# Attention output copied from fixed buffers ahead of the state update, with shorter loads of k and q, in a kernel of attention and two MoE layers

## The chip, the cores and the metric

The kernel runs on one core of one Trainium2 chip, in one launch. Time is device microseconds of one execution of the whole program; before the change the median of 3 runs is 924.24 us (924.11 to 925.05).

## The reference

The first stage is a linear recurrence over a sequence of 768 positions, for 4 batches and 8 heads of 48 dimensions, with a decay `alpha` of its own for each key dimension and position:

```python
def _attn_ref(q, k, v, alpha):
    B, H, S, D = q.shape
    state = np.zeros((B, H, D, D), dtype=np.float32)
    y = np.zeros_like(q)
    for t in range(S):
        state = alpha[:, :, t, :, None] * state + np.einsum('bhd,bhe->bhde', k[:, :, t], v[:, :, t])
        y[:, :, t] = np.einsum('bhd,bhde->bhe', q[:, :, t], state)
    return y
```

Its output, transposed to 3,072 tokens of 384 features, goes through two layers of the form `act(x @ w_in) @ w_out` with 2,048 inner features. The first has a rational function of `h` as `act` (a cubic over `1 + |b0 h| + |b1| h²`), the second `h * cos(h)`. The change touches the first stage alone.

## The kernel before

**Attention in steps.** The sequence is cut into 6 chunks of 128 positions; with 4 batches that makes 24 steps u (chunk u // 4, batch u % 4). One tile of a step holds all 8 heads: 4 head pairs along the free axis, and on the 128 rows one head of a pair on rows 0 to 47, the other on rows 64 to 111. Rows 48 to 63 and 112 to 127 are filling. A step loads `a` (the decays), `kq` (k and q together, 128 rows × 1,024 numbers, 512 KB) and `v`. VectorE makes running products `p` of the decays (`decay`, L255) and, from a first guess on ACT (`guess`, L271), their inverse (`inverse0`, `inverse1`, L280 and L288); POOL scales k and q by these (`scale_k` L294, `scale_q` L299). Then:

- PE: `scores` (L307) makes k·q of the chunk in two PSUM tiles; ACT copies them out (`mask0`, L314), POOL zeroes the upper triangle (`mask1`, L319).
- PE: `transposes` (L327) turns k; ACT copies it out as `kt` (`k_out`, L332); PE multiplies it with v into `u` (`update0`, L339); VectorE adds that to the state and decays it by `pc` (`update1`, L349 to L353; `pc` comes from `last_decay`, L264).
- PE: the output is state times q (`y_state`, L372) plus scores times v (`y_scores`, L382), in one PSUM bank `b1`; ACT copies it to SBUF (`y_out`, L393) and SP stores it to DRAM as two DMAs of 48 rows (`y_store`, L399), from where the layers load it as `x`.

**Order of the work.** Every engine works through its instructions in the order in which they are written. The turns n = −3 to 24 (L1238) call `attention(n)` (L403), which writes pieces of several steps: scores, mask0 and transposes of step n; k_out, mask1, y_state, y_scores, update0 and y_out of step n−1; the decays of step n+3; the second half of the update of step n−2. Turn n also issues on SP, in this order, `a` of step n+5 (two DMAs of 48 rows, L233), `kq` of n+3 (L229), `v` of n+2 (L224), a piece of the weights (L149) and the store of step n−2 (L399). SP's DMAs have eight completion counters that are used in turn, so an issue waits until the eighth DMA before it has landed. In between ACT, VectorE and POOL unpack the weights (`tick`: L68, L69, L73, L74; `w_hi` L188; `w_lo` L198). From turn 20 (`LEAD`) on the two layers run beside the last attention steps.

**Buffers.** `temp(tag)` (L92) hands out buffers of a pool in turn; the tag `g` has four. In the attention stage `kt` (L331) and the output copy `yo` (L390) of each step both come from it, two copies a step. In 13 of the steps 0 to 19 (3 to 6, 9 to 13, 16 to 19) `yo` gets the buffer that `kt` of its own step has just left, in the others one that an earlier store has read. A writer of a buffer waits until everything that read it is done: the readers of a `kt` are the matmuls of `update0`, those of a `yo` are the two DMAs of its store. For u from 20 on `yo` comes from another pool. The `kq` tiles are five fixed buffers used in turn.

Of the kernel before, what the change touches and what calls it, by code (L numbers as in the profile page):

```python
# [16 lines left out]
B, H, S, D = 4, 8, 768, 48  # L17
DM, DFF = 384, 2048
NC, C = 6, 128
HP = 4  # L20
# [19 lines left out]
def attn_then_two_moe(ctx, tc, kqT, aT, vP, w1i, w1o, ma, mb, w2i, w2o, out):  # L40
    nc = tc.nc
# [50 lines left out]
    def temp(tag, dtype=F32, shape=(128, TB)):  # L92

        bufs = {"z": 3, "ah": 2, "g": 4, "hi": 3, "lo": 3}[tag]
        return el.tile(list(shape), dtype, tag=tag, name=tag, bufs=bufs)

    def bank(tag, shape=(128, TB), dtype=F32):

        return ps.tile(list(shape), dtype, tag=tag, name=tag)
# [28 lines left out]
    LEAD = NU - 4  # L128
# [52 lines left out]
    def w_hi():  # L181
        while to_hi:
            m, s, i = w = to_hi.pop(0)
            at = early(m, s, i)
            hi = ws[s][i][:, 0]
            if at is not None:
                hi = kq_t[at % 3][:, 1].rearrange("p a b -> p (a b)")[:, :DM].bitcast(F32R)
            nc.scalar.activation(out=hi, in_=stage[w], func=AF.Copy)  # L188
            to_lo.append((w, hi))
# [21 lines left out]


    U = {}

    def load(u, name):


        if u >= NU:
            return
        c, b = divmod(u, B)  # L220
        ts = {"a": a_t, "kq": kq_t, "v": v_t}[name]
        t, src = ts[u % len(ts)], {"a": aT, "kq": kqT, "v": vP}[name][c, b]
        if name == "v":
            nc.sync.dma_start(out=t[:, :H * D], in_=src)  # L224
        elif u == 0 and name == "a":
            for cs in (slice(0, HP + HP // 2 * C), slice(HP + HP // 2 * C, HP * (C + 1))):
                nc.sync.dma_start(out=t[:, cs], in_=src[:, cs])
        elif u < len(ts) or name == "kq":
            nc.sync.dma_start(out=t, in_=src)  # L229
        else:  # L230
            for j in range(2):
                js = slice(64 * j, 64 * j + D)
                nc.sync.dma_start(out=t[js], in_=src[js])  # L233
        d = U.setdefault(u, {})
        if name == "kq":
            d["k"], d["q"] = t[:, 0], t[:, 1]
        else:
            d[name] = t


    def parts(u):
        return [slice(0, HP // 2), slice(HP // 2, HP)] if u == 0 else [slice(0, HP)]
# [6 lines left out]
    def decay(u):  # L249
        d = U[u]  # L250
        d["p"] = in_p.tile([128, HP, C], F32, tag="p", name="p")
        a = d.pop("a")
        first, rest = a[:, :HP].unsqueeze(2), a[:, HP:].rearrange("p (a b) -> p a b", a=HP)
        for hs in parts(u):
            nc.vector.tensor_tensor(out=fresh[:, hs, 0:1], in0=first[:, hs], in1=fresh[:, hs, 1:2], op=ALU.max)  # L255
            nc.vector.tensor_tensor_scan(
                d["p"][:, hs].rearrange("p a b -> p (a b)"), rest[:, hs].rearrange("p a b -> p (a b)"),
                fresh[:, hs].rearrange("p a b -> p (a b)"), 0.0, ALU.mult, ALU.max,
            )

    def last_decay(u):
        d = U[u]
        d["pc"] = in_p.tile([128, HP, 1], F32, tag="pc", name="pc", bufs=6)
        nc.vector.tensor_tensor(out=d["pc"], in0=d["p"][:, :, C - 1:], in1=fresh[:, :, 1:2], op=ALU.max)  # L264


    def guess(u):
        d = U[u]
        d["r"] = bank("b1" if u == 1 else "r0", (128, HP, C))
        for hs in parts(u):  # L270
            nc.scalar.activation(out=d["r"][:, hs], in_=d["p"][:, hs], func=AF.Ln)  # L271
            nc.scalar.activation(out=d["r"][:, hs], in_=d["r"][:, hs], func=AF.Exp, scale=-1.0)
# [3 lines left out]
    def inverse0(u, hs):  # L276
        d = U[u]
        if hs.start == 0:
            d["m"] = temp("ah", shape=(128, HP, C))
        nc.vector.scalar_tensor_tensor(  # L280
            d["m"][:, hs], d["p"][:, hs], RANGE, d["r"][:, hs], ALU.min, ALU.mult, accum_out=sums(1, u, hs)
        )

    def inverse1(u, hs):
        d = U[u]
        if hs.start == 0:
            d["n"] = temp("z", shape=(128, HP, C))
        nc.vector.scalar_tensor_tensor(  # L288
            d["n"][:, hs], d["m"][:, hs], -2.0, d["r"][:, hs], ALU.add, ALU.mult, accum_out=sums(0, u, hs)
        )  # L290

    def scale_k(u, hs, eng):
        d = U[u]
        eng.tensor_tensor(out=d["k"][:, hs], in0=d["k"][:, hs], in1=d["n"][:, hs], op=ALU.mult)  # L294

    def scale_q(u):
        d = U[u]
        for hs in parts(u):
            nc.gpsimd.tensor_tensor(out=d["q"][:, hs], in0=d["q"][:, hs], in1=d["p"][:, hs], op=ALU.mult)  # L299

    def scores(u):
        d = U[u]
        d["sc"] = [ps_acc.tile([128, HP, C], F32, tag=f"acc{j}", name=f"sc{j}") for j in range(2)]
        for hp in range(HP):
            for j in range(2):
                js = slice(64 * j, 64 * j + D)
                nc.tensor.matmul(d["sc"][j][:, hp, :], d["k"][js, hp, :], d["q"][js, hp, :], start=True, stop=True)  # L307

    def mask0(u):
        d = U[u]  # L310
        d["s"] = []
        for j, sc in enumerate(d.pop("sc")):
            s = temp(("hi", "lo")[j], shape=(128, HP, C))
            nc.scalar.activation(out=s, in_=sc, func=AF.Copy, scale=-1.0)  # L314
            d["s"].append(s)

    def mask1(u):
        for s in U[u]["s"]:
            nc.gpsimd.affine_select(  # L319
                s, s, pattern=[[0, HP], [1, C]], compare_op=ALU.is_ge, fill=0.0, base=0, channel_multiplier=-1  # L320
            )
# [6 lines left out]

    def k_out(u):
        d = U[u]  # L330
        d["kt"] = temp("g", shape=(128, HP, 128))  # L331
        nc.scalar.activation(out=d["kt"], in_=d.pop("tp"), func=AF.Copy)  # L332

    def update0(u):
# [42 lines left out]
    def y_scores(u):  # L377
        c, b = divmod(u, B)
        d = U[u]
        for hp in range(HP):  # L380
            for j in range(2):
                nc.tensor.matmul(  # L382
                    d["y"][64 * j:64 * j + 64, hp, :], d["v"][:, (2 * hp + j) * D:(2 * hp + j) * D + 64], d["s"][j][:, hp, :],
                    start=not c and hp == 0, stop=True, skip_group_check=True,
                )

    def y_out(u):
        d = U[u]
        if u < NU - B:
            d["yo"] = temp("g", shape=(128, HP, C))  # L390
        else:
            d["yo"] = in_p.tile([128, HP, C], F32, tag="p", name="yo")
        nc.scalar.activation(out=d["yo"], in_=d["y"], func=AF.Copy)  # L393
# [9 lines left out]
    def attention(n, tick):  # L403

        def on(u, more=False):
            return 0 <= u < (NU - B if more else NU)

        whole = slice(0, HP)
        if on(n - 1, True):
            k_out(n - 1)  # L410
        w_hi()

        if on(n):
            scores(n)

        if 0 <= n - 1 < LEAD:
            mask1(n - 1)
        if on(n + 1):
            scale_q(n + 1)

        if on(n + 1):
            if n < 1:
                for hs in parts(n + 1):
                    inverse0(n + 1, hs)
                    inverse1(n + 1, hs)
                    scale_k(n + 1, hs, nc.gpsimd)
            else:
                inverse0(n + 1, whole)
                inverse1(n + 1, whole)
                scale_k(n + 1, whole, nc.vector if n + 2 == NU else nc.gpsimd)  # L430
                tick(0 if on(n + 2) else 1)
        tick(1)
        if on(n + 3):
            decay(n + 3)
        tick(1)
        if on(n - 2, True):
            update1(n - 2, tick)
        tick(1)
        if on(n + 3):
            last_decay(n + 3)  # L440

        if on(n):
            mask0(n)
        if n not in (-1, 0) and on(n + 2):
            guess(n + 2)
        if n in (-2, -1):
            guess(n + 3)

        if on(n - 1):
            y_state(n - 1)  # L450
            y_scores(n - 1)
        if on(n, True):
            transposes(n)
        if on(n - 1, True):
            update0(n - 1)
        if on(n - 1) and n < LEAD:
            y_out(n - 1)
        tick(1 if n < LEAD else 2)
        if on(n) and n >= LEAD:
            mask1(n)  # L460
# [760 lines left out]
    with tc.manual_schedule():  # L1221
        nc.scalar.preload_act_table_set("natural_log_exp_and_others")
        for name, u in (("a", 0), ("a", 1), ("kq", 0), ("kq", 1)):
            load(u, name)
# [239 lines left out]
```

## Time and profile before

| | |
|---|---|
| median of 3 runs | 924.24 us (924.11 to 925.05) |
| the profiled execution, its own time | 924.49 us |
| its span in the profile | 922.8 us |
| PE busy over the span | 895.2 us, 97% |
| ACT, POOL, DVE busy | 697.5, 712.5, 706.6 us (76, 77, 77%) |
| PE's matmul clock, mean of full speed | 0.995 |
| q1, the DMA queue of the program's transfers | 122.95 MB, 41.7% of 16 engines' time |

The busy shares are means over the whole program. Attention takes the first eighth or so of the span and the two layers the rest; these have different limits, so a change in attention has to be read from that stretch alone. The profile names a wait by the instruction that waited and by what ended the wait; times in the trace count from the start of the span.

### The profile page before, as it was taken

To read this page: it belongs to the slowest core of one execution; us is meant where nothing else is said; L and a number is where in the kernel's file an instruction comes from. 1 tells how busy PE (TensorE), PEld (TensorE's weight loads), DVE (VectorE), ACT (ScalarE), POOL (GpSimd) and SP (SyncE) were. 2 spreads that over 40 slices of the span, in tenths; PEclk is the share of its full clock that TensorE was granted. 3 is DMA by queue.
4 is the path that set the end of the run, shared out by engine and by line. 5 is a ranking of instruction groups with operands and counts; after the bars stand their busy time and mean duration, and the time that the engine had idled before them with its cause. 6 is when DMAs were issued, how large, how long until landed. Compare 5 with 4: busy or idle time off the path is not lost.

```text
span 922.8 us, 15700 instructions
## 1 busy us (share of the span) xinstructions
PE 895.2 (97%) x5336; PEld 741.7 (80%) x5336; DVE 706.6 (77%) x1246; ACT 697.5 (76%) x1305; POOL 712.5 (77%) x699
## 2 busy tenths in 40 slices
PE   7888899999999999999999999999999999999996
PEld 6776678888888888888888888878888888888885
DVE  7888979998999989979979967666367554555552
ACT  6998888888789878888878778755577676666653
POOL 6998998998889879889979758758887475665332
PEclk8999999999999999999999999999999999999999
DMA  9999940011124133142157457541243433533432
GB/s 298 315 310 311 329 137 16 28 35 52 68 78 121 43 100 97 46 150 89 34 163 223 140 185 260 195 136 35 69 138 94 154 116 100 171 104 103 138 103 90
DMA packets 64313, 124.04 MB, mean 134 GB/s; under 512 B 7424, under 2 KB 29184, under 8 KB 64224
## 3 DMA queue, kind: packets, MB, share of 16 engines
q1 hardware_dynamic: 64224, 122.95, 41.7%
q8 instruction: 44, 0.72, 0.3%
q14 instruction: 45, 0.37, 0.1%
HBM read 93.04 MB, written 29.88 MB: 133 GB/s over the span
## 4 chain that ended last, share of the span: by engine, by line
PE 86%; DMA 5%; ACT 4%; DVE 2%; issue 1%; POOL 1%; SPq 0%; ACTq 0%; DVEq 0%; POOLq 0%
PE acc L522 28%; PE b L506 28%; PE acc L987 15%; PE b L952 6%; PE r L952 5%; DMA x0d<-g 2%; DMA spare<-w1o 1%; PE b L1131 1%; DMA raw<-w1o 1%; PE sc L307 1%; DMA kq<-kqT 1%; DMA raw<-w1i 1%; ACT st L68 0%; ACT g L332 0%; ACT hi L314 0%
## 5 line engine op out<-in xcount | busy, mean ns | idle before, releaser
L506 PE MATMUL b<-x,w 128*128 128x512 f32 x1143 | 287.6, 396 | 0.2 <-DVE g L575 0.2
L506 PEld LDWEIGHTS b<-x,w 128*128 128x128 f32 x1143 | 214.4, 188 | 52.3 <-DVE g L575 0.6
L522 PE MATMUL acc<-hi,w 128*128 128x512 f32 x738 | 252.7, 396 | 0.0
L557 POOL TENSOR_TENSOR lo<-g,hi 128x512 fp32r<-128x512 f32 x128 | 174.5, 1363 | 69.5 <-ACT hi L552 63.2
L522 PEld LDWEIGHTS acc<-hi,w 128*128 128x128 f32 x738 | 138.7, 188 | 34.1
L1044 POOL TENSOR_TENSOR lo<-g,hi 128x512 fp32r<-128x512 f32 x64 | 83.0, 1297 | 103.8 <-ACT hi L1043 91.8
L522 PE MATMUL acc<-lo,w 128*128 128x512 f32 x369 | 145.6, 395 | 0.0
L552 ACT ACTIVATE hi<-g 128x512 fp32r<-128x512 f32 x128 | 80.8, 631 | 85.3 <-DVE g L588 47.4
L583 POOL TENSOR_TENSOR z<-z,ah 128x512 f32<-128x512 f32 x96 | 126.5, 1318 | 8.0
L987 PE MATMUL acc<-hi,w_out 128*128 128x512 f32 x384 | 130.4, 396 | 0.0
L584 DVE TENSOR_TENSOR g<-g,b 128x512 f32<-128x512 f32 x96 | 65.3, 680 | 26.5 <-ACT g L581 26.1
L522 PEld LDWEIGHTS acc<-lo,w 128*128 128x128 f32 x369 | 69.4, 188 | 16.4
L987 PE MATMUL acc<-lo,w_out 128*128 128x512 f32 x192 | 76.3, 398 | 0.4 <-POOL lo L1044 0.2
L987 PEld LDWEIGHTS acc<-hi,w_out 128*128 128x128 f32 x384 | 68.6, 188 | 9.9
L582 POOL TENSOR_SCALAR z<-ah,cq 128x512 f32<-128x512 f32 x96 | 74.5, 776 | 1.0 <-ACT ah L580 0.9
L581 ACT ACTIVATE g<-b,cq 128x512 f32<-128x512 f32 x96 | 74.6, 777 | 0.0
L588 DVE SCALAR_TENSOR_TENSOR g<-g,cq,r 128x512 f32<-128x512 f32 x96 | 70.8, 737 | 0.1
L575 DVE SCALAR_TENSOR_TENSOR g<-g,cq,b 128x512 f32<-128x512 f32 x96 | 70.6, 735 | 0.0
L592 ACT ACTIVATE r<-z,lnb 128x512 f32<-128x512 f32 x96 | 66.7, 695 | 0.9 <-POOL z L583 0.9
L577 DVE SCALAR_TENSOR_TENSOR r<-z,r 128x512 f32<-128x512 f32 x96 | 65.5, 683 | 0.0
L572 DVE SCALAR_TENSOR_TENSOR z<-z,r 128x512 f32<-128x512 f32 x96 | 64.9, 676 | 0.0
L580 ACT ACTIVATE ah<-b 128x512 f32<-128x512 f32 x96 | 56.4, 588 | 8.0 <-PE b L506 7.0
(192 smaller groups left out, 1823.3 us busy)
## 6 DMA issues: line engine op xcount, KB each, us to landing
w_out<-wd SPq DMA_DIRECT2D x64, 384.0 KB, 3.0
kq<-kqT SPq DMA_DIRECT2D x24, 512.0 KB, 5.4
raw<-w2i SPq DMA_DIRECT2D x16, 384.0 KB, 3.5
w<-wd SPq DMA_DIRECT2D x16, 384.0 KB, 3.3
raw<-w2o SPq DMA_DIRECT2D x16, 384.0 KB, 3.5
wd<-w SPq DMA_DIRECT2D x16, 384.0 KB, 2.6
v<-vP SPq DMA_DIRECT2D x24, 192.0 KB, 5.4
x<-x0d SPq DMA_DIRECT2D x18, 256.0 KB, 3.7
```

Source lines behind the costliest of these rows:

```text
L506: nc.tensor.matmul(h, ws[0][f][:, w, ks], x[:, xx, kk, :], start=i == 0, stop=i == 8)
L522: nc.tensor.matmul(acc[k], ws[1][f][:, w, ks], d[g], start=first and i == 0, stop=last and i == 2)
L552: nc.scalar.activation(out=t["hi"], in_=t["g"], func=AF.Copy)
L557: eng.tensor_tensor(out=t["lo"], in0=t["g"], in1=t["hi"].bitcast(F32), op=ALU.subtract)
L575: nc.vector.scalar_tensor_tensor(g, g, cq[:, 3:4], two["h"], ALU.add, ALU.mult)
L581: nc.scalar.activation(out=g, in_=h, func=AF.Identity, scale=cq[:, 5:6], bias=cq[:, 4:5])
L582: nc.gpsimd.tensor_scalar(zz, ah, cq[:, 1:2], cq[:, 0:1], ALU.mult, ALU.add)
L583: nc.gpsimd.tensor_tensor(out=zz, in0=zz, in1=ah, op=ALU.mult)
L588: nc.vector.scalar_tensor_tensor(g, g, cq[:, 2:3], r, ALU.add, ALU.mult)
L952: nc.tensor.matmul(tile[:, half], w[p], x[q], start=start and i == 0, stop=True, skip_group_check=True)
L987: nc.tensor.matmul(acc[k], item["w"][:, w, ks], item[g], start=first, stop=last)
L1044: nc.gpsimd.tensor_tensor(out=p["lo"], in0=p["g"], in1=p["hi"].bitcast(F32), op=ALU.subtract)
```

## The change

Four things are edited. (1) Four buffers `kept` are taken from the `g` pool once, at the start. (2) `k_out` writes `kept[0]` and `kept[1]` in turn. (3) `y_out` writes `kept[2]` and `kept[3]` in turn (for u below 20), and its call in `attention` stands ahead of `transposes` and `update0`, for n below `LEAD`. (4) The `kq` loads from u = 5 on, that is from the second use of each of the five buffers, load rows 0 to 111 alone (64 + 48); rows 112 to 127 keep what the buffer's first load left there.

```diff
     U = {}
+    kept = [temp("g", shape=(128, HP, C)) for _ in range(4)]
...
-        elif u < len(ts) or name == "kq":
+        elif u < len(ts):
             nc.sync.dma_start(out=t, in_=src)
+        elif name == "kq":
+            rows = slice(0, 64 + D)
+            nc.sync.dma_start(out=t[rows], in_=src[rows])
         else:
...
     def k_out(u):
         d = U[u]
-        d["kt"] = temp("g", shape=(128, HP, 128))
+        d["kt"] = kept[u % 2]
...
     def y_out(u):
         d = U[u]
         if u < NU - B:
-            d["yo"] = temp("g", shape=(128, HP, C))
+            d["yo"] = kept[2 + u % 2]
...
         if on(n - 1):
             y_state(n - 1)
             y_scores(n - 1)
+        if on(n - 1) and n < LEAD:
+            y_out(n - 1)
         if on(n, True):
             transposes(n)
         if on(n - 1, True):
             update0(n - 1)
-        if on(n - 1) and n < LEAD:
-            y_out(n - 1)
```

In the changed kernel `k_out` is L336, `mask0` L318, `y_out` L397, the `kq` load L233 and `y_store` L403.

On every engine the instructions stand in the same order before and after. What differs is what they wait for. ACT in turn 17, before: `hi` and `lo` are the two score copies of step 17, `r0` the guess of step 19, `g_1605` the output copy of step 16, `x` a piece of layer input, `g_1616` the `kt` copy of step 17, `w1_7` and `st` weights. In brackets stand the counters waited for: PE, DVE, Pool and Activation are engines, DMAHW0 to DMAHW7 the eight counters of SP's DMAs.

```order
L314 ACTIVATE hi_1567<-sc0_1538 128x512 [waits PE_49]
L314 ACTIVATE lo_1569<-sc1_1539 128x512 [waits PE_49]
L271 ACTIVATE r0_1571<-p_1476 128x512 [waits DVE_49]
L272 ACTIVATE r0_1571<-r0_1571 128x512 [waits Activation_49]
L393 ACTIVATE g_1605<-b1_1574 128x512 [waits PE_49]
L635 ACTIVATE x_794<-x_794 128x512 [waits DMAHW4_49]
L332 ACTIVATE g_1616<-b0_1591 128x512 [waits DMAHW7_49,DMAHW0_49]
L188 ACTIVATE w1_7_128<-st_104 128x384 [waits DVE_49]
L68 ACTIVATE st_104<-spare_141 128x384 [waits DMAHW6_49,Pool_49]
```

The same place after:

```order
L318 ACTIVATE hi_1538<-sc0_1509 128x512 [waits PE_49]
L318 ACTIVATE lo_1540<-sc1_1510 128x512 [waits PE_49]
L275 ACTIVATE r0_1542<-p_1449 128x512 [waits DVE_49]
L276 ACTIVATE r0_1542<-r0_1542 128x512 [waits Activation_49]
L397 ACTIVATE g_144<-b1_1545 128x512 [waits DMAHW7_49,DMAHW6_49,PE_49]
L639 ACTIVATE x_784<-x_784 128x512 [waits DMAHW4_49]
L336 ACTIVATE g_143<-b0_1563 128x512 [waits PE_49]
L188 ACTIVATE w1_7_128<-st_104 128x384 [waits DVE_49]
L68 ACTIVATE st_104<-spare_141 128x384 [waits Pool_49]
```

The output copy of step 16 waited for PE up to the last matmul of `update0(16)`; now it waits for PE up to `y_scores(16)`, and on two DMA counters for the landing of store(14), which read `kept[2]` last. The `kt` copy of step 17 waited for the landing of store(13), and by way of it for all that PE had done; now it waits for the transposes of step 17. On SP one turn (turn 13: the loads of `kq` of step 16 and `v` of step 15, a weight piece, the store of step 11) reads, before:

```order
L229 DMA kq_99<-kqT 128x1024 [waits DMAHW5_49,PE_49,Pool_49]
L224 DMA v3_103<-vP 128x384 [waits DMAHW6_49,PE_49]
L149 DMA spare_141<-w1o 128x768 [waits DMAHW7_49]
L399 DMA x0d_57<-g_1193 48x512 [waits DMAHW0_49,Activation_49]
L399 DMA x0d_57<-g_1193 48x512 [waits DMAHW1_49]
```

and after:

```order
L233 DMA kq_99<-kqT 112x1024 [waits DMAHW5_49,PE_49,Pool_49]
L225 DMA v3_103<-vP 128x384 [waits DMAHW6_49,PE_49]
L149 DMA spare_141<-w1o 128x768 [waits DMAHW7_49]
L403 DMA x0d_57<-g_145 48x512 [waits DMAHW0_49,Activation_49]
L403 DMA x0d_57<-g_145 48x512 [waits DMAHW1_49]
```

The `kq` load has 112 rows; the store of the step reads a fixed buffer and stands where it stood, behind the turn's loads.

## Rows read from the trace of the kernel before

**Rows 1.** The page: busy time by engine, and PE and DMA in 40 slices.
```profile
PE 895.2 (97%) x5336; PEld 741.7 (80%) x5336; DVE 706.6 (77%) x1246; ACT 697.5 (76%) x1305; POOL 712.5 (77%) x699
...
PE   7888899999999999999999999999999999999996
...
DMA  9999940011124133142157457541243433533432
```

**Rows 2.** Stretches: us; busy PE, PEld, DVE, ACT, POOL; PEclk, DMA share, GB/s.
```profile
16.00:116.00 100.00, 84.94 (x1283) 70.24 (x1279) 87.34 (x219) 92.09 (x191) 92.95 (x100) 1.00 0.97 319
117.00:218.00 101.00, 100.80 (x551) 80.61 (x548) 93.39 (x138) 86.88 (x157) 94.44 (x86) 1.00 0.17 50
20.00:25.00 5.00, 3.98 (x58) 3.16 (x56) 4.86 (x12) 4.97 (x11) 4.71 (x6) 1.00 1.03 359
30.00:35.00 5.00, 5.00 (x86) 4.20 (x87) 4.31 (x12) 4.94 (x11) 5.00 (x7) 1.00 0.89 263
```

**Rows 3.** 16 to 116 us: waits (us, times, longest), and two lines' groups.
```profile
ACT g L393 <- PE u L339: 4.9, 8, 1.2
...
POOL hi L319 <- ACT hi L314: 3.8, 3, 1.6
...
L339 PE MATMUL u<-v,g 128*64 128x48 f32 x320 | 13.4, 225 | 14.0 <-DVE pc L264 7.1 <-DVE s L353 4.4 <-DVE s L349 2.5
```

**Rows 4.** Timeline around 98 us: start, us, engine; in brackets the idle time before.
```profile
97.88 0.15 DVE L264 TENSOR_TENSOR pc<-p,r 128x4 f32<-128x4 f32 x1
...
98.11 0.67 PE L339 MATMUL u<-v,g 128*64 128x48 f32 x16 [0.84 <-DVE pc L264]
```

**Rows 5.** Timeline of ACT, the output copies of steps 2, 11, 16, 17, 18.
```profile
26.18 0.59 ACT L393 ACTIVATE g<-b 128x512 f32<-128x512 f32 x1
...
71.38 0.60 ACT L393 ACTIVATE g<-b 128x512 f32<-128x512 f32 x1 [0.33 <-PE u L339]
...
98.82 0.60 ACT L393 ACTIVATE g<-b 128x512 f32<-128x512 f32 x1 [1.21 <-PE u L339]
...
104.14 0.60 ACT L393 ACTIVATE g<-b 128x512 f32<-128x512 f32 x1 [0.33 <-PE u L339]
...
109.15 0.60 ACT L393 ACTIVATE g<-b 128x512 f32<-128x512 f32 x1 [0.54 <-PE u L339]
```

**Rows 6.** Timeline of SP: issues of the stores 0, 9, 14, 16, and of kq(20).
```profile
20.20 1.28 SPq L399 DMA_DIRECT2D x0d<-g  x2
...
68.62 1.68 SPq L399 DMA_DIRECT2D x0d<-g  x2
...
95.63 0.81 SPq L399 DMA_DIRECT2D x0d<-g  x2
...
98.52 0.36 SPq L229 DMA_DIRECT2D kq<-kqT  x1
...
104.63 0.81 SPq L399 DMA_DIRECT2D x0d<-g  x2
```

**Rows 7.** DMA issues near 20, 69, 96, 105 us: KB each, median us to landing.
```profile
x0d<-g SPq DMA_DIRECT2D x2, 96.0 KB, 6.2
...
x0d<-g SPq DMA_DIRECT2D x2, 96.0 KB, 5.5
...
x0d<-g SPq DMA_DIRECT2D x2, 96.0 KB, 5.1
...
x0d<-g SPq DMA_DIRECT2D x2, 96.0 KB, 5.4
```

**Rows 8.** DMA from 20 to 110 us: all packets.
```profile
DMA packets 14171, 28.29 MB, mean 314 GB/s; under 512 B 2305, under 2 KB 6064, under 8 KB 14155
```

**Rows 9.** Timeline of POOL, the first mask of step 19.
```profile
113.05 0.63 POOL L319 TENSOR_SCALAR_AFFINE_SELECT hi<-hi 128x512 f32<-128x512 f32 x1 [1.64 <-ACT hi L314]
```

## The prediction

> **What bounds the kernel now.** I read the page first: PE works 97% of the span, but the slices show it in two parts, a first eighth in which PE is at 7 to 8 tenths while the DMA row stands at 9, and a long rest in which PE stands at 9 and DMA at 0 to 7 [rows 1]. The change lies wholly in the first part, so next I cut the time into stretches: from 16 to 116 us PE is busy 84.9 of 100 us, ACT 92.1, POOL 93.0, and the DMA engines 97%; from 117 us on PE is busy 100.8 of 101 us [rows 2]. So the attention turns are paced by the transfers, with ACT and POOL close behind, and what they save or lose shifts everything after one for one, because PE then has no idle time in which to swallow it. Third the waits and lines of the turns [rows 3]: ACT's copy of an output (L393) waits 4.9 us in 8 pieces for PE's `update0` (L339), which itself waits 14.0 us for VectorE, half of it for L264; and POOL waits 3.8 us for ACT's L314, which stands behind that copy.
>
> **Part 1, the wait taken away.** No instruction changes its place on any engine; the edit changes what `y_out` waits for. Before, `y_out(u)` takes in most steps the `g` buffer that `update0(u)` has just read (in the rest one that store(u−3) has read); after, it needs only the end of `y_scores(u)` and a store. The 8 waits are 4.9 us in all. A gain can't pass the idle time that they leave on ACT, so the ends of this part are 0 (the next bound takes it all) and −4.9. How one case works: `update0(16)` starts at 98.11 us, 0.84 us late, because VectorE gets to L264 only at 97.88 [rows 4], and `y_out(16)` starts at 98.82 after 1.21 us of idle time [rows 5]. What ACT does behind it (L332, the weight words, the next L314) would come earlier by that much, and POOL's L319 with it.
>
> **Part 2, the wait put in its place.** With two fixed buffers for the outputs `y_out(u)` must wait until store(u−2) has landed. SP issues a store two turns after its copy and it lands over 5 us later, so this is close. I take the second of a store's two DMAs to go out half the pair's issue time behind the first. Store(0): 20.20 + 0.64 + 6.2 = 27.0 us, and `y_out(2)` started at 26.18, 0.9 us earlier. Store(9): 68.62 + 0.84 + 5.5 = 75.0 against `y_out(11)` at 71.38, 3.6 us earlier. Store(14): 95.63 + 0.4 + 5.1 = 101.1 against `y_out(16)` at 98.82, 2.3 us earlier. Store(16): 104.63 + 0.4 + 5.4 = 110.4 against `y_out(18)` at 109.15, 1.3 us earlier [rows 5 to 7]. These are the first, the longest and the last two that count; it is so in 16 of the 17 steps 2 to 18. So the wait for `update0` doesn't simply go: a wait for a store comes, and queued behind it on ACT are `k_out(u+1)` (on which the next `update0` hangs), the weight words and the next L314, for which POOL waits. `k_out`'s own fixed buffers I cost at nothing: before, it waited for a store four steps old, long landed; now it waits for the transposes alone.
>
> **Part 3, the short loads.** 19 of the 24 kq loads (from u = 5 on) move 112 rows instead of 128: 16 rows × 4,096 B = 65.5 KB less each, of 512 KB. DMA is the bound of this stretch, so bytes are time: at 314 GB/s, the mean of 20 to 110 us [rows 8], the saving is s = 65.5 KB ÷ 314 GB/s = 0.209 us a load; at 359 GB/s, the best stretch I looked at [rows 2], 0.183. The trace has no 112-row load, so I bound s from both sides: above by 0.209; below by a load whose bytes go at the worst rate I found, 448 KB at the 263 GB/s of 30 to 35 us [rows 2], 1.744 us against 512 KB at 314 GB/s, 1.670 us, which is s = −0.075. I take s = 0.2, the stretch's own mean rate, because that mean already holds transfers on all kinds of row counts at 97% busy engines, the 48-row loads and stores among them. The Trainium skill speaks to this from one side: "DMA: Bandwidth & Descriptors", section "Why a DMA increments its semaphore by 16 and not by 1", splits a transfer over the largest number of engines, at most 16, that divides its slowest dimension; for 112 that is 16 engines with 7 rows each where 128 gives 8, and by it s would be whole. No row here shows it.
>
> **The sum.** From u = 2 on the outputs hang on the stores, the stores on SP's queue, and that on the DMA engines, so I follow this chain. Ahead of store(14)'s landing lie 15 short loads (kq 5 to 19; kq 20 is issued at 98.52, behind store(14) [rows 6]). It lands at 101.1 − 15 s, and there `y_out(16)` starts. The two turns from it to `y_out(18)` took 109.15 − 98.82 = 10.33 us, of which 0.33 + 0.54 were waits for `update0` [rows 5]; without these, 9.46. So `y_out(18)` starts at 101.1 + 9.46 − 15 s = 110.56 − 15 s, against 109.15: a change of +1.41 − 15 s. The other way in, store(16) at 110.4 less 17 short loads, gives 1.25 − 17 s, which is earlier and doesn't decide. With s = 0.2 it is +1.4 − 3.0 = **−1.6 us**. Behind `y_out(18)` it isn't lost: POOL's 1.64 us of idle time for ACT's L314 at 113.05 [rows 9] says that POOL there follows ACT, and from 117 us on PE is full. So the whole −1.6 goes to the end: 924.49 for the profiled execution (its span of 922.8 and 1.7 us around it) becomes 922.9; the median of three runs is 924.24, 0.25 lower, so **922.6 us**.
>
> **The rivals.**
> A, *the full gain*: the stores land in time, because 4% fewer bytes shorten the queue of transfers that makes up most of a landing's 5.1 to 6.2 us [rows 7], for every transfer alike. Then the 4.9 us go whole: 924.2 − 4.9 = 919.3. For it: POOL's idle time in the stretch is 7.0 us (100 − 92.95 [rows 2]), so there is room. Against it: the stores are late by 2 us and more, and all of that has to go.
> B, *slower*: the short loads aren't cheaper, and the store's landing decides. Its place is `y_out(u)` behind store(u−2) at L397, with ACT's queue standing. Its price is +1.4 at s = 0 and +1.41 + 15 × 0.075 = +2.5 at s = −0.075: 925.6 to 926.8. It decides from s below 0.09, where 15 s is 1.41. For it: the engines moved 263 GB/s at a DMA share of 0.89 and 359 at 1.03 [rows 2], a quarter less for a share a seventh lower, so their time isn't bytes alone. Against it: over 90 us the engines stood at 97% and moved all that the turns ask for, and less of the same kind at that mean is less time. [...]
> C, *covered*: the turns are set by POOL at 93% and by VectorE's lateness, the stores land just in time, and of the waits only the last, 0.54 us before `y_out(18)` [rows 5], is really won: 924.24 − 0.54 = 923.7. For it: `update0` stays late, 14.0 us in all [rows 3], and of ACT's 4.9 us only 3.8 show on POOL. Against it: DMA, the busiest, gets less to do.
> That the change doesn't do what it says is not open: in the order `y_out(16)` stands without `update0`, and the kq loads with 112 rows.
>
> **How the numbers follow.** Forecast 0.5 (−1.6, give or take 1.0 for s from 0.13 to 0.27), A 0.12, B 0.2, C 0.18. I count as the same what lies within 0.2%, 1.85 us, about what a measurement of this kernel can tell from no change. Faster: 0.22 of the forecast's 0.5, all 0.12 of A, 0.02 of C, together 0.36. Slower: 0.17 of B, which straddles the bound, and 0.02 of the others, 0.19. The same: the rest, 0.45. The range reaches from A's end to B's far end, 919.3 to 926.8, and leaves out what lies beyond these; the forecast's own range is 921.6 to 923.6.
>
> **What would show it.** In the waits of 16 to 116 us ACT's copy, now L397, no longer stands behind `update0`; in its place stands a DMA `x0d<-g`, in many pieces of up to 3 us (forecast, B) or hardly at all (A, C). The kq loads show 448 KB, and the DMA share stays near 0.97 over a stretch that is shorter by the forecast's 1.6 us. `y_out(18)` starts at 107.5 us (forecast), 104.3 (A), 110.6 or later (B), 108.6 (C). PE must still be full after 117 us; if it shows idle time there, the step that hands the stage's gain to the end is wrong. The forecast is wrong if the landing of kq loads doesn't get earlier although they are shorter, or if `y_out` waits for stores and the time falls all the same by over 3 us: then the stores hung not on the transfers, as I take it, but on something that the change itself makes earlier.

## The result and the profile after

The change made the kernel slower: 930.72 us median (928.83 to 933.82, 6 runs) against 924.56 us of the kernel before in the same comparison, a ratio of 1.0067 (95% interval 1.0046 to 1.0088), so +6.2 us (+4.3 to +8.1). The prediction was −1.6 us, and 930.72 lies above its range too. The profiled execution is the slowest of the six, 933.82 us with a span of 932.0, 9.2 us longer than the span before; so its rows show the causes somewhat larger than the median has them.

Where it came from is read in the order of the prediction. The waits of ACT's copy from 16 to 116 us in the changed kernel (us, times, longest):

```profile
ACT g L397 <- DMA x0d<-g: 8.0, 6, 3.8
...
POOL hi L323 <- ACT hi L318: 4.2, 6, 1.5
...
ACT g L397 <- PE u L343: 2.9, 3, 1.8
```

The 4.9 us behind `update0` [rows 3] became 8.0 us behind the store, and the 2.9 us that the profile still puts down to `update0` are taken for the store's too: the copy no longer waits for `update0`, and a wait for several counters is named by the one that came last in the records. POOL waits for ACT's L318 as long as before, 4.2 us against 3.8. So the wait in place of the wait is there, and it is larger than the one removed. The stretches of the changed kernel (us; busy PE, PEld (PE's loading of weights), DVE, ACT, POOL; PEclk, DMA share, GB/s):

```profile
16.00:116.00 100.00, 84.05 (x1196) 69.64 (x1193) 81.06 (x204) 84.78 (x176) 87.74 (x93) 0.93 1.02 289
...
30.00:39.00 9.00, 7.91 (x70) 6.63 (x70) 4.90 (x13) 7.66 (x17) 6.23 (x8) 0.51 0.81 218
117.00:122.00 5.00, 3.23 (x56) 2.63 (x53) 4.96 (x8) 4.26 (x9) 4.91 (x5) 1.00 0.96 299
122.00:127.00 5.00, 5.00 (x33) 3.71 (x33) 4.31 (x8) 2.26 (x5) 5.00 (x5) 0.66 0.30 86
```

In the first of them the DMA engines are busier than before, 1.02 against 0.97, and move less, 289 against 319 GB/s, while ACT fell from 92.1 to 84.8 and POOL from 93.0 to 87.7 [rows 2]. The transfers still run at a share of 0.96 from 117 to 122 us, and there PE has work for 3.2 of 5 us. Two more lines of the DMA view say it in one number. From 20 to 110 us, after (queue: packets, MB, share of 16 engines):

```profile
DMA packets 13377, 25.86 MB, mean 287 GB/s; under 512 B 2231, under 2 KB 5904, under 8 KB 13362
...
q1 hardware_dynamic: 13362, 25.68, 101.1%
...
kq<-kqT SPq DMA_DIRECT2D x17, 448.0 KB, 6.0
```

and before, the same stretch:

```profile
q1 hardware_dynamic: 14155, 28.09, 95.4%
...
kq<-kqT SPq DMA_DIRECT2D x18, 512.0 KB, 5.4
```

Share × 90 us ÷ MB is the time of all 16 engines for a megabyte: 0.954 × 90 ÷ 28.09 = 3.06 us before, 1.011 × 90 ÷ 25.68 = 3.54 us after. (The share adds up the times of packets, so it can pass 100%; what makes a packet's time longer no row shows.) The loads are shorter, and a megabyte takes 16% longer. The kq loads land later after their issue, 6.0 us, than the longer ones did, 5.4.

The timeline shows the first of the store's waits and what it drags behind it (start, us, engine; in brackets the idle time before):

```profile
22.43 1.26 SPq L403 DMA_DIRECT2D x0d<-g  x2
...
26.47 1.16 PE L311 MATMUL sc<-kq 48*128 48x128 f32 x16
...
30.40 0.60 ACT L397 ACTIVATE g<-b 128x512 f32<-128x512 f32 x1 [3.78 <-DMA x0d<-g]
...
31.09 0.45 PE L386 MATMUL b<-hi,v 128*64 128x128 f32 x1 [3.46 <-POOL kq L298]
...
35.08 2.08 PE L311 MATMUL sc<-kq 48*128 48x128 f32 x16
...
42.03 0.60 ACT L397 ACTIVATE g<-b 128x512 f32<-128x512 f32 x1 [1.82 <-PE u L343]
...
115.50 0.60 ACT L397 ACTIVATE g<-b 128x512 f32<-128x512 f32 x1
...
123.30 0.58 ACT L397 ACTIVATE g<-b 128x512 f32<-128x512 f32 x1
```

Store(0) goes out 2.2 us later than before (22.43 against 20.20 [rows 6]) and lands at about 30.3; `y_out(2)` starts at 30.40, 4.2 us later than before (26.18 [rows 5]). PE waits with it: `y_scores(3)` writes the one bank `b1` from which `y_out(2)` reads, and starts at 31.09, just behind the copy's end at 31.00 (POOL's L298, which the profile names, had ended at 30.24). After these 3.46 us without work PE's granted clock stands at half, 1.2 of 2.4 GHz, from 30 to 39 us (0.51 above), and the same 16 matmuls of `scores` take 2.08 instead of 1.16 us. `y_out(18)` comes at 115.50 instead of 109.15, +6.35 us. But `y_out(4)` is already 7.0 us late (42.03 against 35.01 before): in this execution the loss was made by 42 us, where the first store's wait and the half clock lie, and it did not grow over the short loads that came after.

### The profile page after: what moved, and what is told of

Read it like the earlier page. It is cut to its first block, busy times and chain, and to the rows that moved or that the text cites. A ratio compares the mean times of both kernels' runs of the same rounds, so it can differ in the third digit from the quotient of the medians.

```text
span 932.0 us, 15681 instructions
## 1 busy us (share of the span) xinstructions
PE 902.8 (97%) x5336; PEld 747.6 (80%) x5336; DVE 708.2 (76%) x1246; ACT 698.3 (75%) x1305; POOL 715.4 (77%) x699
## 4 chain that ended last, share of the span: by engine, by line
PE 84%; DMA 5%; ACT 4%; DVE 2%; issue 1%; POOL 1%; SPq 1%; ACTq 0%; DVEq 0%; POOLq 0%
PE b L510 28%; PE acc L526 26%; PE acc L991 15%; PE b L956 6%; PE r L956 5%; DMA kq<-kqT 2%; DMA raw<-w2o 1%; DMA x0d<-g 1%; PE b L1135 1%; DMA spare<-w1i 1%; PE sc L311 1%; ACT hi L318 1%; PE b L386 1%; ACT b L69 0%; ACT lo L318 0%
```

## The experiments

All ratios are to the kernel before, with a 95% interval; a unit of 0.001 is 0.92 us. Each changed kernel has 5 to 12 executions.

**1. The two halves of the change, each alone.** Short loads only:

```diff
-        elif u < len(ts) or name == "kq":
+        elif u < len(ts):
             nc.sync.dma_start(out=t, in_=src)
+        elif name == "kq":
+            rows = slice(0, 64 + D)
+            nc.sync.dma_start(out=t[rows], in_=src[rows])
```

> The kernel before with the 112-row kq loads alone (19 loads), k_out and y_out as before. The change measured +6.2 us. Theory S (the stores decide: y_out behind store(u-2) sets the pace): without that wait the short loads can only save, 0 to -4 us. Theory L (the short loads decide: engine time for a megabyte in 20 to 110 us went from 3.06 to 3.54 us, worked out as DMA share x 90 us / MB): +4 to +8 us, engine time for a megabyte stays near 3.5, and the mean rate near 287 GB/s. If both share it: about +3 us.

Measured 1.0032 (1.0020 to 1.0043), +3.0 us. The change without these lines (fixed buffers and early copy, kq loads of 128 rows):

```diff
+    kept = [temp("g", shape=(128, HP, C)) for _ in range(4)]
...
-        d["kt"] = temp("g", shape=(128, HP, 128))
+        d["kt"] = kept[u % 2]
...
-            d["yo"] = temp("g", shape=(128, HP, C))
+            d["yo"] = kept[2 + u % 2]
...
+        if on(n - 1) and n < LEAD:
+            y_out(n - 1)
         if on(n, True):
             transposes(n)
...
-        if on(n - 1) and n < LEAD:
-            y_out(n - 1)
```

> The change without its short loads: four fixed buffers and the early y_out, kq loads of 128 rows. Theory S: +4 to +7 us, y_out of nearly all steps starting 0.1 us behind a store's landing. Theory L: within -2 to +1.5 us of the kernel before (my sum for s = 0 was +1.4), engine time for a megabyte back at 3.06 us. If both share it: about +3 us.

Measured 1.0035 (1.0021 to 1.0049), +3.2 us. Neither theory alone survives: each half costs about 3 us, and 3.0 + 3.2 is the change's 6.2. The DMA view from 20 to 110 us of the short loads alone, then of the copy alone:

```profile
q1 hardware_dynamic: 13445, 25.88, 100.5%
```

```profile
q1 hardware_dynamic: 13973, 27.56, 94.3%
```

Worked out as above: 3.50 us for a megabyte with the short loads, 3.08 with full ones. The dearer transfers belong to the short loads alone. There the loss shows as late kq loads, for which POOL waits 6.6 us where it waited 1.2 before (waits, 16 to 116 us):

```profile
POOL kq L302 <- DMA kq<-kqT: 6.6, 9, 1.6
```

The copy alone shows the store's wait without them (waits, 16 to 116 us):

```profile
ACT g L394 <- DMA x0d<-g: 4.7, 3, 1.9
```

and, in the stretch from 36 to 56 us, PE busy all but 0.2 us at a clock of 0.70, while ACT and POOL have work for 13.9 and 13.2 of 20 us:

```profile
36.00:56.00 20.00, 19.81 (x229) 16.40 (x226) 12.18 (x33) 13.87 (x30) 13.15 (x15) 0.70 0.93 306
```

**2. The store's wait taken away.** Three buffers for the outputs and one for `kt`, so that `y_out(u)` waits for store(u−3); with the short loads and with full ones:

```diff
-        d["kt"] = kept[u % 2]
+        d["kt"] = kept[0]
...
-            d["yo"] = kept[2 + u % 2]
+            d["yo"] = kept[1 + u % 3]
```

> The change with one fixed buffer for k_out and three for y_out, so that y_out waits for store(u-3) instead of store(u-2), short loads kept. Theory S: the wait for stores goes, faster than before by 1 to 5 us. Theory L: as slow as the change or less by the store's wait, +3 to +6 us; ACT waits for x0d<-g under 2 us in 16 to 116 us.

> One fixed buffer for k_out, three for y_out, and kq loads of 128 rows: y_out waits neither for update0 nor for a store that is late. Theory S: faster than before by 1 to 4 us. Theory L: faster by 0 to 4 us as well (the 4.9 us of waits for update0 at most); together with the run that has two buffers for y_out and full loads it prices the store's wait alone.

Measured 1.0038 (1.0022 to 1.0055), +3.5 us, with the short loads; 1.0001 (0.9989 to 1.0014), no difference, with full ones. So with full loads a third output buffer takes away the whole loss of the copy's half (3.2 us with two, 0 with three): it is the store's wait, with PE's pause and the half clock that hang on it. The third buffer doesn't shrink the loss of the loads. The second number also bears on the change's aim: `y_out` no longer waits for `update0`, and nothing is won. That kernel's waits, 16 to 116 us:

```profile
POOL kq L300 <- DMA kq<-kqT: 4.5, 6, 1.2
ACT st L68 <- DMA spare<-w1o: 4.4, 3, 2.5
...
ACT g L394 <- PE u L340: 2.0, 2, 1.4
...
ACT g L333 <- PE u L340: 1.4, 3, 0.7
```

and in those of the kernel before, which had these two small:

```profile
POOL kq L299 <- DMA kq<-kqT: 1.2, 1, 1.2
...
ACT st L68 <- DMA spare<-w1o: 0.7, 2, 0.5
```

This kernel isn't free of such waits. The 2.0 us before `y_out` (L394) are a store's again, of store(u−3): store(9) goes out at 70.96 us and takes 5.5 us to land, and `y_out(12)` starts at 76.95. The 1.4 us before `k_out` (L333) are new: with a single `kt` buffer `k_out` waits for `update0`. Besides, ACT waits 3.7 us longer for weights (4.4 − 0.7) and POOL 3.3 us longer for kq (4.5 − 1.2): what runs ahead meets the transfers. In the kernel of section 3 neither `y_out` nor `k_out` is named as waiting for `update0`, its waits for the same weights and kq are 4.5 and 2.9 us, and nothing is won there either. VectorE holds a part, too. With three buffers and full loads `y_out(18)` starts 1.86 us earlier than before (107.29), but `update0(18)`, which waits for VectorE's `pc` (L265, 0.87 us), only 0.56 us earlier (107.88), and `update0(19)` 0.19 us later (113.48). So the wait for `update0` was for the most part slack against transfers and VectorE; how much against which is read from these rows and was not tested.

**3. The store issued earlier.** The copy's half with two buffers, but the store at the head of the turn's issues on SP:

```diff
+            if n >= 2:
+                y_store(n - 2)
             if n >= -1:
                 load(n + 5, "a")
...
-                if n >= 2:
-                    y_store(n - 2)
```

> The change without its short loads, with the store of step n-2 written at the head of turn n's issues on SP instead of behind the turn's loads, so that it goes out 1 to 2 us sooner. If the lateness of store(u-2) is this part's cause: ACT's waits for x0d<-g in 16 to 116 us fall from 4.7 us to under 2, PE's pause at 27 us goes and with it the half clock of 28 to 48 us, and the time is within -1 to +1.5 us of the kernel before. If something else of this edit costs (the order of copies, the fixed buffers): still +2.5 to +4 us.

Measured 1.0013 (1.0003 to 1.0022), +1.2 us instead of +3.2, with this left of the wait:

```profile
ACT g L394 <- DMA x0d<-g: 1.3, 1, 1.3
```

The lateness of store(u−2) is confirmed from the other side, with the two buffers kept. As expected the half clock of 28 to 48 us didn't come; another did, from 82 to 95 us, behind pauses of PE of under 0.8 us, so a part of what remains may be that (its stretch from 76 to 96 us):

```profile
76.00:96.00 20.00, 18.63 (x194) 15.20 (x190) 16.20 (x40) 15.10 (x32) 18.34 (x20) 0.66 0.95 314
```

**4. What makes the short loads dear: bytes or rows.** The same 448 KB as 128 rows of 896 numbers; and the 96 rows that hold data, as two DMAs of 48:

```diff
+            flat = "p a b c -> p (a b c)"
+            nc.sync.dma_start(out=t.rearrange(flat)[:, :7 * C], in_=src.rearrange(flat)[:, :7 * C])
```

> The kernel before, its kq loads from u = 5 as 128 rows x 896 columns, the same 448 KB as the 112-row loads (the q of the fourth head pair is not loaded and keeps old values). Theory R (it is the 112 rows that make every transfer dear, not the bytes): engine time for a megabyte in 20 to 110 us back near 3.06 us, and no slower than before, 0 to -3 us. Theory B (packets or bytes as such, or running ahead, make it dear): +2 to +4 us as with the 112 rows, 3.5 us for a megabyte.

```diff
-        elif u < len(ts) or name == "kq":
+        elif u < len(ts):
             nc.sync.dma_start(out=t, in_=src)
         else:
             for j in range(2):
                 js = slice(64 * j, 64 * j + D)
                 nc.sync.dma_start(out=t[js], in_=src[js])
```

> The kernel before, its kq loads from u = 5 as two DMAs of 48 rows each (384 KB in all, the filling rows left out, as the decays are loaded). Theory R in the form that a transfer of 48 rows, too, goes across the others: 3.3 us for a megabyte or more, the bytes saved (2.4 MB of 28) given back, -1 to +4 us. If only the 112 are bad: -3 to -6 us, engine time for a megabyte near 3.06.

Measured 0.9996 (0.9982 to 1.0011) and 1.0075 (1.0050 to 1.0100, +6.9 us). The queue's lines, 20 to 110 us, first of the 128 rows with fewer columns, then of the two times 48:

```profile
q1 hardware_dynamic: 14413, 27.45, 94.2%
```

```profile
q1 hardware_dynamic: 12842, 23.59, 94.8%
```

That is 3.09 and 3.62 us for a megabyte. With all 128 rows the bytes saved cost nothing, but they win nothing either, −0.4 us (−1.7 to +1.0): the DMA share falls to 0.94, and ACT and POOL are busy 90 and 92 of 100 us, about as before:

```profile
16.00:116.00 100.00, 86.57 (x1263) 71.33 (x1262) 85.85 (x217) 90.19 (x187) 92.07 (x99) 0.97 0.94 306
```

With a quarter of the kq bytes left out by rows, the kernel gets slower, and by more than was expected of any case. Whether the missing rows or the split does it was then still open, so the whole 512 KB was loaded as two DMAs of 64 rows, and the change's 112 rows as 64 and 48:

```diff
+            for rows in (slice(0, 64), slice(64, 128)):
+                nc.sync.dma_start(out=t[rows], in_=src[rows])
```

> The kernel before, its kq loads from u = 5 as two DMAs of 64 rows (512 KB in all, no row left out). Theory P (what makes transfers dear is that a load isn't one DMA over all 128 rows, so that its rows fall otherwise on the 16 engines than those of the other loads): engine time for a megabyte in 20 to 110 us 3.3 us or more, +2 to +6 us. Theory G (it is the missing rows 112 to 127 that make it dear): 3.06 to 3.15 us, 0 to +1.5 us for the 19 more issues on SP.

```diff
+            for rows in (slice(0, 64), slice(64, 64 + D)):
+                nc.sync.dma_start(out=t[rows], in_=src[rows])
```

> The kernel before, its kq loads from u = 5 as two DMAs of 64 and 48 rows, together the change's 112 rows (448 KB). Theory P: 3.3 us for a megabyte or more, +2 to +7 us. Theory G: as one DMA of 112 rows, 3.5 us and +3 us. If only a row count that is no power of two is dear: between the two, +1 to +3 us.

Measured 1.0141 (1.0114 to 1.0167, +13.0 us) and 1.0107 (1.0080 to 1.0135, +9.9 us), both beyond what theory P expected. The lines of the first, with its wait for kq from 16 to 116 us, then of the second:

```profile
q1 hardware_dynamic: 12529, 23.86, 97.0%
...
kq<-kqT SPq DMA_DIRECT2D x28, 256.0 KB, 5.4
...
POOL kq L302 <- DMA kq<-kqT: 17.6, 14, 2.2
```

```profile
q1 hardware_dynamic: 13113, 24.62, 99.2%
```

3.66 and 3.63 us for a megabyte. No row is left out in the first, and it is the slowest of all. Common to every dear form is that a kq load isn't one DMA over all 128 rows. The price isn't the whole of the loss: two times 64 rows was 10 us slower than the 112 rows, with the engines' share lower (97.0 against 100.5%). The two-DMA forms also use two of SP's eight counters a load, which may account for the rest; that wasn't tested. The Trainium skill, "DMA: Bandwidth & Descriptors", section "The descriptor swizzle", says that in a transfer to 128 partitions each engine writes a port of its own. That the other shapes are dear because they lose this order is a guess: no run here shows ports or which engine moved what.

**5. The clock.** Matmuls on constants ahead of `scores` keep PE busy; their results are overwritten. First 14 at u = 4 and 4 at each other u to 19, on the change and on the kernel before:

```diff
+        for i in range({4: 14}.get(u, 4) if 3 < u < LEAD else 0):
+            nc.tensor.matmul(d["sc"][0][:, i % HP, :], ident, ident, start=True, stop=True)
```

> The change, with matmuls on constants put on PE ahead of scores(u) for u = 4 to 19, 14 of them at u = 4 and 4 at each other (their results are overwritten). Theory C (a pause of PE lets the granted clock fall to half, and the half clock then makes PE the bound for whole turns; that is most of the loss): the clock of 28 to 58 us stays at 1.0 and the time falls by 2 to 5 us against the change, to +1 to +4 us over before. Theory D (the DMA's dearer bytes and the store's wait are the loss, the clock only shows them): as slow as the change, +5 to +8 us, although the clock stays up.

> The kernel before with the same added matmuls, the price of the filling alone: PE has 15 of 100 us free in 16 to 116 us and the filling is worked out at about 12 us (74 matmuls at 0.165 us, the time of one of L327's), so 0 to +2 us; its clock was 1.0 in all stretches after 15 us and gains nothing.

Measured 1.0069 (1.0050 to 1.0088) and 1.0061 (1.0043 to 1.0080). The second was expected at 0 to +2 us and came at +5.6; from 16 to 116 us it has PE all but full:

```profile
16.00:116.00 100.00, 97.35 (x1367) 82.95 (x1368) 82.28 (x209) 86.33 (x178) 90.16 (x96) 1.00 0.96 312
```

So this filling made PE the bound, and the pair says nothing on the clock. It was tried again with 14 matmuls at u = 4 alone, on the copy's half and on the kernel before:

> The change without its short loads (the run that was +3.4 us), with 14 matmuls on constants ahead of scores(4) alone, where PE paused behind the first store's landing and its granted clock then stood at half from 27 to 48 us. Theory C (the clock makes most of this part's loss): the clock stays at 1.0 there, and against the control with the same filling the loss is 0 to +1.5 us. Theory W (the wait itself, 1 to 4 us at the first store and some more later, is the loss): +2.5 to +4 us against the control.

> Control: the kernel before with the same 14 matmuls ahead of scores(4). Their price alone; one turn's PE work grows by about 1 to 2 us where PE has some slack: 0 to +1.5 us. Both theories expect the same.

Measured 1.0037 (1.0025 to 1.0050) and 1.0020 (1.0007 to 1.0033). The difference, 0.0017 or 1.6 us, lies between what the two theories expected, and the intervals overlap. In the first of them the clock didn't fall after the first pause, and the copy then waited longer for stores than without the filling, 7.8 us instead of 4.7:

```profile
ACT g L396 <- DMA x0d<-g: 7.8, 7, 3.0
```

Last, the kernel with three output buffers and full loads, with 8 such matmuls ahead of scores(8) and scores(14), where its clock had fallen for some 5 us each. Its stretches without the filling:

```profile
36.00:56.00 20.00, 17.07 (x226) 13.82 (x224) 14.93 (x39) 15.77 (x34) 18.20 (x19) 0.91 1.00 334
...
76.00:96.00 20.00, 17.85 (x252) 14.85 (x252) 16.51 (x44) 17.40 (x37) 19.32 (x21) 0.91 1.00 320
```

What was expected of the filling:

> The kernel with three buffers for y_out and full loads (0.0 us against before), with 8 matmuls on constants ahead of scores(8) and scores(14) each, where PE paused for late weights and kq loads and the clock then stood at half for some 5 us. Theory C: the clock of 46 to 52 and 85 to 89 us stays at 1.0 and the time falls to -1 to -3 us against before. Theory W: 0 to +1 us, the added matmuls only cost. If the DMA engines alone set the pace, no change either: 0.

Measured 0.9998 (0.9985 to 1.0010), against 1.0001 without the filling. With it the clock is whole in both:

```profile
36.00:56.00 20.00, 17.67 (x262) 14.86 (x260) 16.25 (x43) 17.63 (x37) 18.37 (x21) 1.00 0.98 318
...
76.00:96.00 20.00, 16.93 (x255) 14.30 (x255) 15.49 (x39) 17.79 (x37) 19.00 (x21) 1.00 0.99 321
```

So a fallen clock of that length cost nothing that can be measured in this kernel. For the longer ones its share of the loss stays open, in both halves: 9 us in the profiled execution of the change, 20 in that of the copy alone, and 14 in that of the short loads alone (85 to 99 us, a clock of 0.51, PE busy 13.5 of 14 us). The 13 us in the kernel with the store issued earlier went with a loss of 1.2 us in all. None of the versions beat the kernel before by more than their interval.

## Why the prediction was wrong

**What bounds the kernel.** Half right. Dearer transfers lengthen the turns, so their time is a bound close at hand. It isn't the only one: the kq loads of 128 rows with fewer columns moved the forecast's 448 KB at the price of before, and the time stayed (0.9996). ACT and POOL, "close behind" in the prediction, were as near.

**Part 1, −4.9 to 0.** The end that came is 0: with the wait for `update0` gone, waits for weights and kq and VectorE's lateness took its place. The prediction held this only as rival C, and there named POOL and VectorE as the cover, not the transfers.

**Part 2, the store's wait.** The mechanism was right and was found in the rows before: `y_out(u)` stands behind store(u−2). Its size was too small: the sum at s = 0 is +1.4 us, and the copy alone, with full loads, measured +3.2. What failed is where the wait decides. The prediction has `y_out` late in 16 of 17 steps and lets the landing of store(14) and store(16), at their issue times of before, set the end. In the copy alone three copies wait for a store, those of steps 2, 5 and 11, in the change six and perhaps three more, and in neither run does `y_out(16)` or `y_out(18)`: in the copy alone `y_out(16)` starts at 104.86 us, 6.0 later than before, but store(14) goes out at 97.39, only 1.8 later, and has landed by then. So the waits come early, and a copy that is late meets a store that has landed. What makes the turns late is what the first waits drag behind them. In the profile of the copy alone `y_out` is 2.0 us late at step 3 and 7.0 at step 6, of which 1.6 us is a wait for a store; the half clock of 28 to 48 us lies there, and its share is open. The prediction also missed a queue: it listed what waits behind the copy on ACT, but not PE, whose next `y_scores` needs the bank that the copy empties. In the change the first case, priced at 0.9 us, held `y_out(2)` back by 4.2 us, 2.2 of them because store(0) went out later; no copy had yet waited for a store by then, and with three buffers and full loads it went out at 22.10 us too, so that part isn't the wait's doing and its cause is open.

**Part 3, s = 0.2 us.** This is the step that failed, in sign. Its premise that bytes are time at the mean rate fails even at an unchanged price: the loads with fewer columns won 0.4 us (−1.7 to +1.0) where 15 s would be 3.0. And for 112 rows the price doesn't stay. The lower bound of −0.075 was taken from a slow stretch of full loads, which can't show what a load of 112 rows does to the others. Worked out from the run with the short loads alone: what the 90 us from 20 to 110 moved before, less 17 × 65.5 KB, is 26.98 MB; at 1.005 × 90 ÷ 25.88 = 3.495 us a megabyte that takes 94.3 us, against 0.954 × 90 = 85.9 before. That is +8.4 us of engine time for 17 loads, s = −0.5. Of that, 4.6 us went into time in which engines had been idle (their share rose from 95.4 to 100.5% of 90 us); the 3.8 left are near the +3.0 us measured. That the 48-row transfers run in the same mean was no evidence: they were there before the change as after it, beside kq loads over all 128 rows.

**The sum.** The prediction follows one chain, from the short loads through the stores to `y_out(18)`. The runs show two losses that stand apart: the short loads alone, without a store's wait, cost 3.0 us through late kq loads, and the third output buffer didn't shrink that. 1.41 − 15 s with s = −0.5 would be +8.9 us; that `y_out(18)` came +6.35 us in the profiled execution doesn't bear the chain out, for 7.0 us were there at `y_out(4)`.

**"From 117 us on PE is full."** Not so after: the transfers ran to 122 us, PE had 3.2 us of work in five, and from 122 to 127 us its clock was 0.66. The 6.35 us at `y_out(18)` became 9.2 at the span's end, so the loss wasn't handed on one for one but grew. A gain isn't handed on either: with three buffers and full loads `y_out(18)` came 1.86 us earlier, and the span ended at 922.6 us against 922.8.

**The rivals.** B was nearest, slower by short loads that aren't cheaper and by the store's wait; it was given 0.2 and 925.6 to 926.8, too small because its s stopped at −0.075 and its price for the stores at +1.4. The rule of the Trainium skill named for the forecast ("DMA: Bandwidth & Descriptors", section "Why a DMA increments its semaphore by 16 and not by 1") gives 16 engines for 112 rows as for 128. The price of a megabyte was 3.50 against 3.06 us all the same, so this number alone doesn't price a load; no run here shows how many engines took part.

## What to carry to other kernels

Where the transfers are a bound, price a load not by its bytes but by what it does to all the others: a run of another shape (the same bytes as 128 rows of 896 numbers, or all the bytes as two times 64 rows) tells shape from size, and here one DMA over all 128 rows was the cheapest for a megabyte. Before giving an output a fixed pair of buffers, lay its next use beside the landing of its store: where the store lands later than that, the wait comes, and everything that waits for the copy, on other engines too, is late with it. A wait of ACT that goes away is worth only what the next wait leaves of it.

## What the runs showed of the hardware that was not expected

- Engine time for a megabyte in 20 to 110 us: 3.01 to 3.12 us in the eight kernels with kq loads of one DMA over 128 rows (3.09 with fewer columns), 3.43 to 3.54 in the four with 112 rows, 3.62 to 3.66 with two DMAs of 48, 64, or 64 and 48 rows. It is a price on the mixture, and two times 64 rows with nothing left out pay it too. A single execution can escape its cost: the three-buffer kernel with short loads paid 3.43 us in its profiled execution and took 924.15 us, the fastest of nine with a median of 927.55.
- After a pause of PE (3.46 us at 27.6 us in the change) its granted clock stood at half for 9 us although PE was at work again. In the kernel before, none of PE's pauses from 16 to 116 us, the longest 1.2 us, was followed by that. With three output buffers and full loads such stretches came behind pauses of 0.5 to 1.1 us, so the length of one pause doesn't tell; taking these stretches away by filling moved nothing in the time.
